# A gated mix of local attention and a GEGLU: attention's two layout changes, from DVE transposes to DMA transposes

## The chip, the core and the metric

The kernel runs on one core of one Trainium2 chip. The metric is the device time of one execution in microseconds (us), and the time of a version is the median over its runs. Engine names are those of the profile: PE does matmuls, DVE is the vector engine, ACT the scalar engine, POOL the general one, and SP issues DMAs. In profile rows, L844 is line 844 of the kernel.

## The reference

The input x has 2048 rows of 1024 numbers in bf16. Two branches are computed from it and mixed by a gate for each row:

```
g = sigmoid(sum(x * gate_w))                                  # one number a row
qkv = x @ wqkv; 32 heads of 32 numbers
for each row s, head h: keys and values of rows s, s-2, ..., s-14 (8 places, dilation 2)
    attn = softmax(q . k * 32**-0.5), places before row 0 masked
    o = sum(attn * v)
a = o @ wo
b = (gelu(x @ w_gate) * (x @ w_up)) @ w_down                  # 3584 wide
out = g * a + (1 - g) * b
```

## The kernel before, in words

**Tiling.** The 2048 rows go in four chunks of 512, two chunks to a superblock. All large products are made by a seven-product scheme for 2x2 blocks, so weights are needed raw and as sums (forms). PE works in this order: transposes of chunk 0's x, q, k and v of chunks 0 and 1 (L473), the FFN of superblock 0 (L970: 28 columns f, 28 matmuls each), down projection 0 (L1117, 252 matmuls; w_down and wo in one accumulation), q, k and v of chunks 2 and 3 (L609), down projection 1, the FFN of superblock 1, down projections 2 and 3.

**Evacuation in the FFN.** Each f leaves its banks by copies and gelus on ACT (L999, L1024, L1042, L1050, L1058, L1011) and by three DVE operations: L1054 adds two products of the gate path, L1033 two of the up path, L1014 multiplies them into hT. A late L1054 holds the gelu L1058 behind it, and with it all that follows on ACT.

**Attention** is done on DVE, between all this, in eight halves of 256 rows (h = 0 to 7, two to a chunk). Features lie so that each head has four of the 128 partitions, with eight features on each (the eight tiles t). For a half:

- `scores`: for each t, L781 multiplies q by the eight shifted k (128x2048), and L787 sums over t: 8 products and 7 sums. The last sum has the key ("qk", h).
- L844 transposes the 128x2048 sum in blocks of 32x32 (key ("acct", h)). L851 and L854 add the head's four partitions, which now lie side by side, L867 and L874 take the maximum, ACT does the exponential (L880), L867 the sum, L887 the reciprocal, L898 the probabilities in two pieces, and ACT spreads each over its features (L904).
- L913 transposes each piece back (2 x 128x1024). Then, for each t, L922 multiplies by the shifted v, and L930, L935 and L939 sum over the eight places into `qo`, which the down projection reads.

Since the blocks are 32x32, the scores lie as 4 groups of 32 partitions; the gate is kept in that layout too, and L756 copies it into columns of 128 rows (16 small copies in all). For h = 0, 28 memsets (L861) mask the places before row 0.

Five buffers (`xbuf`, 128x2048 each) serve all of this; a product is taken up only while a second buffer is free.

**Order.** One planner (`Weave`) writes the order of every engine at build time. It holds several streams of operations (the main one, loads, forms, `attention`, `scores`), each with a bias, keeps a clock for each engine from the cost written beside each operation, and always emits the head of the stream that could start first by that clock. Each engine then runs its list strictly in order. For a DMA the planner counts the issue on SP or POOL, the bytes over one common pipe, and 2.2 us until the data are there. In `scores`, the products of half h wait for ("acct", h - 1).

**Loads.** All loads are issued by SP in one list. Weights go into a ring of 20 buffers of 128x1024 (L342 for the FFN, L362 for the down projections, L307 for q, k, v): a load waits until PE has read what lay in its buffer. x of chunks 1 to 3 comes by DMA transposes (L313, eight a chunk, 128x512 each); those of chunks 2 and 3 stand in the list of loads behind weight blocks 9 to 12 of the first FFN (L384 to L386).

Of the kernel before, what the change touches and what calls it, by code (L numbers as in the profile page):

```python
# [40 lines left out]
class Weave:  # L41
# [42 lines left out]
    def _emit(self, op, t):  # L84
        cost = op.cost
        if op.eng == "ACT" and op.table is not None and op.table != self.table:
            self.table = op.table
            cost += 1.29
        if op.eng in ("SP", "POOL"):
            nbytes, issue = op.cost  # L90
            self.clk[op.eng] = t + issue
            self.pipe = max(self.pipe, t) + nbytes / self.RATE
            op.end = self.pipe + 2.2
        else:
            self.clk[op.eng] = t + cost
# [41 lines left out]
def kernel(  # L137
# [28 lines left out]
    assert H * DL == P and DL == 4 and KT == 8 and NCH % 2 == 0  # L166
    CW = NWIN * AC // DL
    CB = CW // NWIN
    SB = AC // 32
    HQ = 32 // DL  # L170
    FB = 2
    NBLK = FT // FB
    NW = D // 2
# [136 lines left out]
    def load_x(c, deps):  # L310
        deps = deps + ([[("acct", 1)], [("att", 0)]][c - 2] if c > 1 else [])
        for kt in range(KT):
            yield Op("SP", (P * SC * 2, 1.6), lambda kt=kt: nc.sync.dma_start_transpose(  # L313
                out=xT(c, kt), in_=x[c * SC:(c + 1) * SC, kt * P:(kt + 1) * P]), deps, key=("x", c, kt))

    def load_prep(i0):
        n = min(2, NPREP - i0)
        kind, src, nr = ("d", B_w_down, FH) if i0 < FH else ("o", A_wo, NTH)
        r0 = i0 if kind == "d" else i0 - FH
        si = i0 % 5  # L320

        def fn():
            st = stage(si)
            for h, r in ((0, r0), (1, nr + r0)):
                if kind == "d":
                    v = src[r * P:(r + n) * P, :].rearrange("(k p) (h n) -> p k h n", p=P, h=2)
# [39 lines left out]
    def loads():  # L366
# [14 lines left out]
            yield load_prep(i0)  # L381
        for b in range(2, NBLK):
            yield from load_block(0, b)
            if b >= XB:  # L384
                for c, k0 in ((2, 0), (2, 4), (3, 0), (3, 4))[b - XB:b - XB + 1]:
                    yield from list(load_x(c, []))[k0:k0 + 4]  # L386
        for sup in range(NSUP):
            c0 = 2 * sup
            more = sup + 1 < NSUP
# [319 lines left out]
    def gate(c):  # L709
# [20 lines left out]
        ez = small.tile([P, SC // 32], F32, tag="ez", bufs=2, name="ez")  # L730
        omg = small.tile([P, NST], F32, tag="omg", bufs=3, name="omg")
        gates[c] = (ez, omg, zq)

    def gate_sum(c):
        i, free = bank_take()
        zq = gates[c][2]

        def go():
            for q in range(4):
                nc.tensor.matmul(banks[i][32 * q:32 * (q + 1), 0:SC // 32], lhsT=qsum[:], rhs=zq[:], start=True, stop=True,  # L740
                                 tile_position=(0, 32 * q), skip_group_check=True)
        o = pe(1, go, [("zq", c)] + ([free] if free else []))
        yield o
        e = dve(0.1, lambda: nc.vector.tensor_scalar(out=zq[:], in0=banks[i][:, 0:SC // 32], scalar1=ZMAX, scalar2=-ZMAX,
                                                     op0=ALU.min, op1=ALU.max), [o], key=("zc", c))
        yield e
        bank_give(i, e)

    def gate_tail(c):
        ez, omg, og = gates[c]  # L750

        def tail():
            nc.vector.tensor_scalar(out=og[:], in0=ez[:], scalar1=1.0, scalar2=1.0, op0=ALU.mult, op1=ALU.add)
            nc.vector.reciprocal(out=og[:], in_=og[:])
            for q in range(4):
                nc.vector.tensor_copy(out=omg[32 * q:32 * (q + 1), :],  # L756
                                      in_=og[32 * q:32 * (q + 1), :].rearrange("p (j q) -> p j q", q=4)[:, :, q])
        yield dve(1.2, tail, [("ez", c)], lag=0.6, key=("omg", c))

    accs = {}  # L760

# [3 lines left out]
    def scores():  # L765

        for c in range(NCH):
            q_, k_ = qo[c % 2], kT[c]
            for a in range(SC // AC):
                a0 = a * AC  # L770
                h = (SC // AC) * c + a
                gate_ = [("acct", h - 1)] if h else []
                box, last = {}, {}

                def mult(t):
# [42 lines left out]
    def att_half(c, a, h):  # L818
# [10 lines left out]
        def flat(name):  # L829
            return xbuf[:, box[name], :]  # L830

        def lsb():
            return flat("z").bitcast(F32)[:, 0:CW].rearrange("p (w c) -> p w c", w=NWIN)

# [6 lines left out]
        def attn():  # L841
            return flat("w")[:, 3 * CW:4 * CW].rearrange("p (w c) -> p w c", w=NWIN)

        o = dve(2.24, taking("z", lambda: nc.vector.transpose(out=flat("z"), in_=xbuf[:, accs[h], :])), [("qk", h)],  # L844
                pre=xb_pre(), key=("acct", h))
        yield o
        xb_give(accs[h], o)

# [27 lines left out]
        yield o  # L876
        def exps():
            if a == 0:
                nc.scalar.activation(out=gates[c][0][:], in_=gates[c][2][:], func=ACT.Exp)
# [4 lines left out]
        if a == 0:  # L884
# [4 lines left out]
        o = dve(0.15, lambda: V(out=m4()[:, 2, :].rearrange("p (s h) -> p s h", s=SB),  # L889
                                in0=m4()[:, 1, :].rearrange("p (s h) -> p s h", s=SB),  # L890
                                in1=gates[c][0][:, a * SB:(a + 1) * SB].rearrange("p (s o) -> p s o", o=1)
                                .to_broadcast([P, SB, HQ]), op=ALU.mult), [("ez", c), o])
        yield o
        half = NWIN // 2
        es = []
# [14 lines left out]
        xb_give(box["w"], e)  # L910
        for i in range(2):
            def back(i=i):
                nc.vector.transpose(out=flat("ab")[:, i * n // 2:(i + 1) * n // 2],  # L913
                                    in_=flat("e")[:, i * n // 2:(i + 1) * n // 2])
# [372 lines left out]
```

## Time and profile before

| | |
|---|---|
| median of 5 runs | 732.35 us (731.22 to 733.67) |
| the profiled execution | 731.22 us, of which the span of its instructions is 729.4 us |
| granted PE clock | 1.000 |
| DMA moved | 163.73 MB, mean 224 GB/s |
| L844, a transpose of 128x2048 on DVE | 8 times, 2306 ns |
| L913, a transpose of 128x1024 on DVE | 16 times, 1225 ns |
| L781, L922, products of 128x2048 | 64 times each, 1217 and 1218 ns |
| PE, L970 of the FFN | 1568 matmuls |

The page first gives the busy time of each engine and its share of the span. Then it cuts the span into 40 slices of 18.2 us, with a digit for the tenths in which an engine was busy (9 is 90% or more), and the same for the 16 DMA engines. A row of a group tells the line, the engine, the operation, its tiles and shapes, how often it ran, its busy time and mean duration, and then the idle time of the engine just before it with what ended that time. A row of the waits reads "who <- waited for whom: us in total, times, longest". A row of the timeline gives the start, the duration, the engine, line and operation, and in brackets the engine's idle time before it and what ended it. Durations of neighbours on DVE overlap by some 0.07 us, so 128x2048 operations in a row start 1.14 us apart.

### The profile page before, as it was taken

How to read it: one execution, taken by the hardware profiler on the slowest of the kernel's cores; microseconds unless marked ns; L12 is line 12 of the kernel's file. 1: busy time of each engine (PE TensorE's matmuls, PEld its weight loads, DVE VectorE, ACT ScalarE, POOL GpSimd, SP SyncE). 2: the span in 40 equal slices, each digit the busy share in tenths (PEclk: the TensorE clock that was granted, in tenths of full speed). 3: DMA queues.
4: the chain of work that ended last, by engine and by line, in shares of the span. 5: the costliest groups of instructions: out<-in, count | busy, mean ns of one | idle time of the engine just before them, and what ended most of it. 6: DMA issues, size and time to landing. Idle time of an engine off the chain costs nothing.

```text
span 729.4 us, 9971 instructions
## 1 busy us (share of the span) xinstructions
PE 721.7 (99%) x3397; PEld 355.7 (49%) x3397; DVE 631.2 (87%) x935; ACT 314.6 (43%) x532; POOL 72.2 (10%) x128
## 2 busy tenths in 40 slices
PE   8999999999999999999999998999999999999998
PEld 6666644444444444456665443444444444444443
DVE  2689999999999989999899999999999999969300
ACT  2333455558555561035652113576557654220110
POOL 2234422121210100000000001000000000001000
PEclk9999999999999999999999999999999999999999
DMA  9999965648892769943029999555555544899993
GB/s 304 325 326 352 383 214 163 198 139 214 208 226 77 277 202 321 323 151 115 30 89 305 354 300 340 162 151 155 148 157 146 158 150 146 302 302 335 327 303 102
DMA packets 151507, 163.73 MB, mean 224 GB/s; under 512 B 22944, under 2 KB 112032, under 8 KB 151456
## 3 DMA queue, kind: packets, MB, share of 16 engines
q1 hardware_dynamic: 142624, 135.30, 61.4%
q0 software_dynamic: 8544, 27.27, 10.2%
q8 instruction: 26, 0.43, 0.2%
q10 hardware_dynamic: 288, 0.52, 0.2%
q14 instruction: 25, 0.20, 0.1%
HBM read 129.50 MB, written 28.31 MB: 216 GB/s over the span
## 4 chain that ended last, share of the span: by engine, by line
PE 73%; issue 21%; DVE 2%; ACT 1%; DMA 1%; POOL 1%; POOLq 0%; ACTq 0%
PE ps L970 45%; PE ps L1117 17%; PE ps L473 11%; DVE xbuf L922 1%; POOL out_dram L1144 1%; DMA hT<-in_A_x_dram 0%; DVE xbuf L930 0%; PE ps L1212 0%; DMA out_dram<-ost 0%; DVE xbuf L935 0%; DVE ost L1191 0%; ACT ost L1152 0%; ACT L1058 0%; DVE xbuf L787 0%; PE ps L717 0%
## 5 line engine op out<-in xcount | busy, mean ns | idle before, releaser
L970 PEld LDWEIGHTS <-ring 128*128 128x128 bf16 x1568 | 153.3, 98 | 187.8 <-issue 3.7
L970 PE MATMUL ps<-lend,ring 128*128 128x512 bf16 x896 | 212.3, 379 | 2.2 <-ACT m L1024 2.1
L970 PE MATMUL ps<-tf,ring 128*128 128x512 bf16 x672 | 164.0, 379 | 0.0
L1117 PE MATMUL ps<-ring,hT 128*128 128x512 bf16 x708 | 160.7, 379 | 0.0
L1117 PEld LDWEIGHTS <-hT 128*128 128x128 bf16 x708 | 69.2, 98 | 83.3
L781 DVE TENSOR_TENSOR xbuf<-qo,lend 128x2048 bf16<-128x2048 bf16 x64 | 77.3, 1217 | 2.3 <-ACT lend L495 2.3
L922 DVE TENSOR_TENSOR xbuf<-xbuf,lend 128x2048 bf16<-128x2048 bf16 x64 | 77.4, 1218 | 0.1
L787 DVE TENSOR_TENSOR xbuf<-xbuf 128x2048 bf16<-128x2048 bf16 x56 | 68.2, 1217 | 0.2
L609 PEld LDWEIGHTS <-ring 128*128 128x128 bf16 x336 | 43.9, 131 | 28.9 <-DMA ring<-in_A_wqkv_dram 0.4
L473 PE MATMUL ps<-lend,ring 128*128 128x512 bf16 x256 | 56.0, 380 | 0.2 <-DVE lend L1219 0.2
L999 ACT COPY ps<-ps 128x512 f32<-128x512 f32 x56 | 32.0, 571 | 54.8 <-PE ps L970 54.7
L1152 ACT ACTIVATE ost<-ps,omg 128x512 bf16<-128x512 f32 x16 | 11.0, 688 | 102.5 <-PE ps L1117 99.3
L1042 ACT ACTIVATE gl<-ps 128x512 bf16<-128x512 f32 x56 | 33.5, 598 | 49.8 <-PE ps L970 49.7
L1144 POOL DMA_DIRECT2D out_dram<-ost x24 | 13.0, 542 | 413.4 <-ACT ost L1152 319.4
L1117 PE MATMUL ps<-ring,qo 128*128 128x512 bf16 x192 | 49.3, 379 | 0.0
L473 PEld LDWEIGHTS <-ring 128*128 128x128 bf16 x256 | 36.7, 144 | 18.9 <-DMA hT<-in_B_w_down_dram 0.4
L443 POOL DMA_DIRECT2D fforms<-ring x56 | 30.5, 545 | 131.5 <-DVE ring L435 125.0
L609 PE MATMUL ps<-lend,ring 128*128 128x512 bf16 x192 | 43.5, 379 | 0.0
L1014 DVE TENSOR_TENSOR hT<-hT,gl 128x1024 bf16<-128x1024 bf16 x56 | 38.4, 686 | 5.7 <-ACT hT L1011 4.5
L930 DVE TENSOR_TENSOR xbuf<-xbuf 128x1024 bf16<-128x1024 bf16 x64 | 41.9, 686 | 0.7
L1054 DVE TENSOR_TENSOR u<-ps,u 128x512 f32<-128x512 f32 x56 | 38.4, 685 | 4.2 <-PE ps L970 3.2
L1033 DVE TENSOR_TENSOR hT<-ps,m 128x512 bf16<-128x512 f32 x56 | 38.4, 686 | 4.0 <-PE ps L970 3.9
(106 smaller groups left out, 724.5 us busy)
## 6 DMA issues: line engine op xcount, KB each, us to landing
ring<-dforms SPq DMA_DIRECT2D x112, 256.0 KB, 4.9
ring<-in_B_w_down_dram SPq DMA_DIRECT2D x84, 256.0 KB, 4.3
ring<-in_B_w_gate_dram SPq DMA_DIRECT2D x56, 256.0 KB, 4.9
fforms<-ring POOLq DMA_DIRECT2D x56, 256.0 KB, 4.8
ring<-fforms SPq DMA_DIRECT2D x56, 256.0 KB, 3.9
ring<-in_B_w_up_dram SPq DMA_DIRECT2D x42, 256.0 KB, 3.5
ring<-in_A_wqkv_dram SPq DMA_DIRECT2D x40, 256.0 KB, 4.5
ring<-oforms SPq DMA_DIRECT2D x32, 256.0 KB, 5.6
```

The source lines that it names most:

```text
L473: nc.tensor.matmul(banks[bk][:], lhsT=lhsT, rhs=xT(c, kt), start=(kt == 0), stop=(kt == KT - 1))
L609: nc.tensor.matmul(banks[bk][:], lhsT=lhsT, rhs=rhs[:, kt, :], start=(start and kt == 0), stop=(kt == KH - 1), skip_group_check=True)
L781: V(out=w3(box[t]), in0=q_b, in1=k_w, op=ALU.mult)
L787: V(out=w3(box[0]), in0=w3(box[0]), in1=w3(box[t]), op=ALU.add)
L922: return dve(tt(n), taking(("p", t), lambda: V(out=w3(box["p", t]), in0=w3(box["ab"]), in1=v_w, op=ALU.mult)), [("qkv", c, 2, t), abo] + ( ...
L930: V(out=s4(t)[:, t % 2], in0=w3(box["p", t])[:, 0:4], in1=w3(box["p", t])[:, 4:8], op=ALU.add)
L970: nc.tensor.matmul(banks[bk][:], lhsT=wv[:, k, fl * P:(fl + 1) * P], rhs=rhs[:, k, :], start=(start and k == 0), stop=(k == KH - 1), skip_ ...
L1014: yield dve(tt(2 * SC), lambda f=f: nc.vector.tensor_tensor(out=hT[:, :, f, :], in0=hT[:, :, f, :], in1=gl[f][:].rearrange("p (j s) -> p j ...
L1033: ev[f, "up2"] = dve(tt(SC, True), lambda f=f: nc.vector.tensor_tensor(out=hs(f, 1), in0=v3(banks[Bk[f]][:]), in1=v3(m5[f][:]), op=ALU.add ...
L1042: nc.scalar.activation(out=gl[f][:, SC:2 * SC], in_=banks[A[f]][:], func=ACT.Gelu_apprx_tanh)
L1054: e = dve(tt(SC, True), lambda f=f: nc.vector.tensor_tensor(out=u2[f][:], in0=banks[Dk[f]][:], in1=u2[f][:], op=ALU.add), [o, ev[f, "u2"]])
L1117: nc.tensor.matmul(banks[bk][:], lhsT=l, rhs=wv[:, i, :], start=(start and k == 0), stop=(q == last and i == 1), skip_group_check=True)
```

## The change

- The two layout changes of attention are made by DMA transposes, issued by SP (`turn`): one of 128x2048 as 16 blocks of 128x128, and two of 128x1024 back. L844 and L913 leave DVE. The planner is given an issue of 1.3 to 2.05 us for them and a tail behind the 2.2 us, 8 us in half 0 and 1.1 us in the others.
- A block is now 128x128, so a row s of the half is a partition. The mask of half 0 is 7 memsets, the gate has 4 columns instead of 16 and is made in the layout of the output (`gate_sum` gives each group of 32 partitions its own columns), and L756 is gone.
- The products of half h wait for ("qk", h - 1), the last sum of the half before, and not for its transpose.
- The x loads of chunks 2 and 3 leave the list of loads and form a stream of their own (`late_x`), four at a time behind the same blocks 9 to 12, still on SP.

Lines after the first edit shift by some: the fold is L856, L851 before; the FFN's L1054, L1033 and L1014 are L1058, L1037 and L1018; L922 is L926, L898 is L902; the transposes are L849 and L917; weight loads are L345 and L365.

```
-            op.end = self.pipe + 2.2
+            op.end = self.pipe + 2.2 + (op.tail if op.tail > 1.0 else 0.0)
...
-    SB = AC // 32
-    HQ = 32 // DL
+    SB = AC // P
...
+    def late_x():
+        for i in range(4):
+            yield from list(load_x(2 + i // 2, [("w", 0, XB + i, 3)]))[4 * (i % 2):4 * (i % 2) + 4]
...
             yield from load_block(0, b)
-            if b >= XB:
-                for c, k0 in ((2, 0), (2, 4), (3, 0), (3, 4))[b - XB:b - XB + 1]:
-                    yield from list(load_x(c, []))[k0:k0 + 4]
...
             for q in range(4):
-                nc.tensor.matmul(banks[i][32 * q:32 * (q + 1), 0:SC // 32], lhsT=qsum[:], rhs=zq[:], start=True, stop=True,
+                nc.tensor.matmul(banks[i][32 * q:32 * (q + 1), 0:NST], lhsT=qsum[:],
+                                 rhs=zq[:].rearrange("p (j q) -> p j q", q=4)[:, :, q], start=True, stop=True,
                                  tile_position=(0, 32 * q), skip_group_check=True)
...
-            nc.vector.tensor_scalar(out=og[:], in0=ez[:], scalar1=1.0, scalar2=1.0, op0=ALU.mult, op1=ALU.add)
-            nc.vector.reciprocal(out=og[:], in_=og[:])
-            for q in range(4):
-                nc.vector.tensor_copy(out=omg[32 * q:32 * (q + 1), :],
-                                      in_=og[32 * q:32 * (q + 1), :].rearrange("p (j q) -> p j q", q=4)[:, :, q])
-        yield dve(1.2, tail, [("ez", c)], lag=0.6, key=("omg", c))
+            nc.vector.tensor_scalar(out=omg[:], in0=ez[:], scalar1=1.0, scalar2=1.0, op0=ALU.mult, op1=ALU.add)
+            nc.vector.reciprocal(out=omg[:], in_=omg[:])
+        yield dve(0.3, tail, [("ez", c)], lag=0.6, key=("omg", c))
...
-                gate_ = [("acct", h - 1)] if h else []
+                gate_ = [("qk", h - 1)] if h else []
...
+        def rows(name):
+            return flat(name).rearrange("p (b s) -> p b s", s=P)
+
+        def turn(cols, fn, deps, **kw):
+            return Op("SP", (P * cols * 2, max(1.3, cols / 1000.0)), fn, deps, tail=8.0 if h == 0 else 1.1, lag=1.0, **kw)
...
-        o = dve(2.24, taking("z", lambda: nc.vector.transpose(out=flat("z"), in_=xbuf[:, accs[h], :])), [("qk", h)],
-                pre=xb_pre(), key=("acct", h))
+        o = turn(n, taking("z", lambda: nc.sync.dma_start_transpose(out=rows("z"), in_=xbuf[:, accs[h], :])), [("qk", h)],
+                 pre=xb_pre(), key=("acct", h))
...
-                for q in range(4):
-                    for wi in range(1, NWIN):
-                        nc.vector.memset(lsb()[32 * q:32 * q + DIL * wi, wi, 0:HQ], NEG)
-            o = dve(2.0, mask, [o])
+                for wi in range(1, NWIN):
+                    nc.vector.memset(lsb()[0:DIL * wi, wi, 0:H], NEG)
+            o = dve(0.5, mask, [o])
...
             def back(i=i):
-                nc.vector.transpose(out=flat("ab")[:, i * n // 2:(i + 1) * n // 2],
-                                    in_=flat("e")[:, i * n // 2:(i + 1) * n // 2])
-            o = dve(1.16, taking("ab", back) if i == 0 else back, [es[i]], lag=0.6, pre=xb_pre() if i == 0 else None)
+                nc.sync.dma_start_transpose(out=rows("ab")[:, i * NWIN:(i + 1) * NWIN],
+                                            in_=flat("e")[:, i * n // 2:(i + 1) * n // 2])
+            o = turn(n // 2, taking("ab", back) if i == 0 else back, [es[i]], pre=xb_pre() if i == 0 else None)
...
-    w.run([(0.0, main()), (0.0, loads()), (0.1, wforms()), (0.1, x_forms()), (0.1, qkv_forms()), (0.15, preps()), (0.3, attention()), (0.5, scores())])
+    w.run([(0.0, main()), (0.0, loads()), (0.0, late_x()), (0.1, wforms()), (0.1, x_forms()), (0.1, qkv_forms()), (0.15, preps()), (0.3, attention()), (0.5, scores())])
```

More of the change, by code (lines that the diff above doesn't have):

```diff
@@ L729, in gate @@
         yield e
-        ez = small.tile([P, SC // 32], F32, tag="ez", bufs=2, name="ez")
+        zc = small.tile([P, NST], F32, tag="zc", bufs=2, name="zc")
+        ez = small.tile([P, NST], F32, tag="ez", bufs=2, name="ez")
         omg = small.tile([P, NST], F32, tag="omg", bufs=3, name="omg")
-        gates[c] = (ez, omg, zq)
+        gates[c] = (ez, omg, zq, zc)
     def gate_sum(c):
         i, free = bank_take()
-        zq = gates[c][2]
+        zq, zc = gates[c][2:4]
         def go():
             for q in range(4):
-                nc.tensor.matmul(banks[i][32 * q:32 * (q + 1), 0:SC // 32], lhsT=qsum[:], rhs=zq[:], start=True, stop=True,
+                nc.tensor.matmul(banks[i][32 * q:32 * (q + 1), 0:NST], lhsT=qsum[:],
+                                 rhs=zq[:].rearrange("p (j q) -> p j q", q=4)[:, :, q], start=True, stop=True,
                                  tile_position=(0, 32 * q), skip_group_check=True)
@@ L743, in gate_sum @@
         yield o
-        e = dve(0.1, lambda: nc.vector.tensor_scalar(out=zq[:], in0=banks[i][:, 0:SC // 32], scalar1=ZMAX, scalar2=-ZMAX,
+        e = dve(0.1, lambda: nc.vector.tensor_scalar(out=zc[:], in0=banks[i][:, 0:NST], scalar1=ZMAX, scalar2=-ZMAX,
                                                      op0=ALU.min, op1=ALU.max), [o], key=("zc", c))
@@ L749, in gate_tail @@
     def gate_tail(c):
-        ez, omg, og = gates[c]
+        ez, omg = gates[c][0:2]
         def tail():
-            nc.vector.tensor_scalar(out=og[:], in0=ez[:], scalar1=1.0, scalar2=1.0, op0=ALU.mult, op1=ALU.add)
-            nc.vector.reciprocal(out=og[:], in_=og[:])
-            for q in range(4):
-                nc.vector.tensor_copy(out=omg[32 * q:32 * (q + 1), :],
-                                      in_=og[32 * q:32 * (q + 1), :].rearrange("p (j q) -> p j q", q=4)[:, :, q])
-        yield dve(1.2, tail, [("ez", c)], lag=0.6, key=("omg", c))
+            nc.vector.tensor_scalar(out=omg[:], in0=ez[:], scalar1=1.0, scalar2=1.0, op0=ALU.mult, op1=ALU.add)
+            nc.vector.reciprocal(out=omg[:], in_=omg[:])
+        yield dve(0.3, tail, [("ez", c)], lag=0.6, key=("omg", c))
     accs = {}
@@ L878, in exps @@
             if a == 0:
-                nc.scalar.activation(out=gates[c][0][:], in_=gates[c][2][:], func=ACT.Exp)
+                nc.scalar.activation(out=gates[c][0][:], in_=gates[c][3][:], func=ACT.Exp)
             nc.scalar.activation(out=lsb(), in_=lsb(), func=ACT.Exp, scale=scale)
@@ L891, in att_half @@
                                 in1=gates[c][0][:, a * SB:(a + 1) * SB].rearrange("p (s o) -> p s o", o=1)
-                                .to_broadcast([P, SB, HQ]), op=ALU.mult), [("ez", c), o])
+                                .to_broadcast([P, SB, H]), op=ALU.mult), [("ez", c), o])
         yield o
```

## The prediction

> **What bounds the kernel.** I read the page first, then who made PE wait, then the timeline around the one long wait, then the rows of the transposes that are there already. PE is the bound:
>
> ```profile
> span 729.4 us, 9971 instructions
> ...
> PE 721.7 (99%) x3397; PEld 355.7 (49%) x3397; DVE 631.2 (87%) x935; ACT 314.6 (43%) x532; POOL 72.2 (10%) x128
> ...
> DVE  2689999999999989999899999999999999969300
> ...
> DMA  9999965648892769943029999555555544899993
> ```
>
> PE is busy for 99% of the span, and DVE, at 87%, has no slack in most slices between the second and the 36th. DMA is full in the first 90 us and from slice 21 to 24 and 35 to 38. All of PE's waits:
>
> ```profile
> PE ps L970 <- ACT m L1024: 2.1, 1, 2.1
> PE ps L279 <- DVE hT L277: 1.2, 1, 1.2
> PE ps L1212 <- DMA hT<-in_A_x_dram: 0.6, 1, 0.6
> PE ps L473 <- DVE lend L1219: 0.2, 1, 0.2
> ```
>
> The last three lie in the start, which the change leaves alone. So one wait of 2.1 us is all that faster attention can give back. Its place, in order of time:
>
> ```profile
> 454.14 0.68 DVE L1054 TENSOR_TENSOR u<-ps,u 128x512 f32<-128x512 f32 x1
> ...
> 454.86 0.63 ACT L1058 ACTIVATE gl<-u 128x512 bf16<-128x512 f32 x1 [3.76 <-DVE u L1054]
> ...
> 455.40 0.57 ACT L1024 COPY m<-ps 128x512 f32<-128x512 f32 x1
> ...
> 456.01 0.38 PE L970 MATMUL ps<-lend,ring 128*128 128x512 bf16 x1 [2.06 <-ACT m L1024]
> ```
>
> At the start of the second FFN DVE is still multiplying values (L922 to L939 of half 4), so FFN's own L1054 comes late, ACT is held 3.76 us behind it, and PE stands 2.06 us. This also gives a tolerance: 3.76 - 2.06 = **1.7 us** of lateness on DVE in the FFN cost PE nothing.
>
> **What goes.** The transposes on DVE:
>
> ```profile
> L913 DVE STREAM_TRANSPOSE xbuf<-xbuf 128x1024 bf16<-128x1024 bf16 x16 | 19.2, 1225 | 4.0 <-ACT xbuf L904 4.0
> ...
> L844 DVE STREAM_TRANSPOSE xbuf<-xbuf 128x2048 bf16<-128x2048 bf16 x8 | 18.4, 2306 | 0.1
> ```
>
> That is 37.6 us. The 16 copies of L756 (160 ns) are 2.6 us; 28 memsets of L861, 0.75 us together, become 7, about 0.6 us. DVE loses 40.8 us of 631.2, some 4.7 us a half. None of it is on PE's path, except through the wait at 454 us: by then four and a half halves are done, so some 20 us of DVE work are gone ahead of it. The gate's narrower operations (16 to 4 columns) are too few to count; PE has as many instructions as before, in the same order.
>
> **What comes: 24 DMA transposes on SP.** Each has two parts, an issue on SP and a landing. The trace has no transpose from SBUF, and none this large. The nearest rows are the loads of x, 128x512 from HBM, a quarter of a turn of 2048 columns:
>
> ```profile
> 187.87 6.38 SPq L313 DMA_TRANSPOSE lend<-in_A_x_dram  x4
> ...
> L313 SPq DMA_TRANSPOSE lend<-in_A_x_dram x24: 1124/1282/2587, 25.9 to 217.7; - x24
> ...
> DMA to landing us min/median/max: 2.5/5.1/8.0
> ```
>
> Bounds for a turn of 2048 columns, issue to landing: at least 2.5 us (the quickest of a quarter of its size); at most 6.38 - 1.28 + 5.1 = 10.2 us, as if it were four in a row. It is nearest in bytes to the four, but has one issue instead of four: I take 8 us. For the pair of 1024 (L917 in the new code): 2.5 to 1.28 + 8.0 = 9.3 us after the first's issue; I take 1.28 + 5.1 = 6.4.
>
> [...]
>
> **Does DVE wait for a landing?** DVE runs in order, so a fold (L856 new) or a value product (L926) that waits also holds FFN's evacuations behind it. From the order of the changed kernel I summed DVE's work between the last sum of products (L786) and the fold, with the present rows (1.14 us a 2048-wide operation, 0.6 a 1024-wide one). Halves 0 to 7: 11.9, 8.9, 14.6, 40, **4.6**, 30, **7.0**, **1.8** us. Against 8 us, halves 4, 6 and 7 are short. Half 4 stands in the down projection, with no FFN evacuation behind it: 3.4 us of DVE idling, paid from the 20 us freed. Half 6 is 1.0 short, under the tolerance. Half 7 is short on paper by 6.2, but PE paces what stands around it: the evacuation behind the fold is due 6.05 us after the one ahead of it (one f of the FFN, 28 matmuls of 0.216), so it is late by 8 + 0.6 - 6.05 = 2.5 us at most, 0.8 over the tolerance, and by less for every moment that the last sum ends ahead of that first evacuation. For the way back, from the second probability product (L902) to L926: 14.8, 9.4, 7.2, 10.2, 9.9, 8.1, 8.1, 0 us, against a spread on ACT (1.05) and 6.4: 7.5. Half 2 is 0.3 short, in a down projection. Half 7 idles for all of it, with nothing of FFN behind it; its results (L939, the last at 669.7 us now) are read by down projection 3, whose 252 matmuls of 0.216 end at 725.8 and so begin at 671. I cost all this at 0.
>
> **SP's queue.** Behind each waiting turn stand the weight loads. In a down projection a ring buffer is freed in the second half of a product (18 of 36 matmuls) and is needed again two products on, 72 x 0.216 - 3.9 = 11.7 us later; a load lands in 5.5 us at the median there (391 to 445 us). So SP may be held 6.2 us at no cost; in the FFN, where a product's weights serve two f, it is more. A turn or a pair keeps SP issuing for four quarters at most, 6.4 us: it fits, just. The x loads of chunk 3 (8 x 1.28 = 10.3 us) move from 200 to 218 us into the first down loads, among which SP now waits 24.2 us for PE (230 to 262 us): 0. If that cover were gone they would cost up to 10.3 - 6.2 = 4 us.
>
> **DMA.** What the turns take of the engines, from three stretches (the last columns are DMA share and GB/s):
>
> ```profile
> 145.00:163.00 18.00, 18.00 (x85) 8.22 (x84) 17.62 (x22) 10.08 (x18) 2.90 (x6) 1.00 0.44 135
> 176.00:194.00 18.00, 18.00 (x85) 8.18 (x84) 17.85 (x27) 11.87 (x20) 2.71 (x5) 1.00 1.03 212
> ...
> 391.00:445.00 54.00, 54.00 (x252) 24.50 (x251) 53.28 (x74) 9.24 (x16) 3.79 (x7) 1.00 0.99 329
> ```
>
> Eight x transposes raise the share from about 0.5 to 1.03 over 18 us, some 1.1 us each, so a turn of 2048 takes up to 4.5 us of all engines. In 391 to 445 us, already at 0.99, one full turn and one pair fall: loads land up to 4.5 us later, inside the 6.2 us. 0, but thin.
>
> **Waiting for products only.** The next half's products (L780) no longer wait for the turn; that wait cost nothing before, since the transpose followed the last sum on DVE (0.1 us idle). It fills the landing. Taking it as 0 to 1 us, I take 0.
>
> **Sum.** The profiled execution took 731.22 us, span 729.4, and was the fastest of five; median 732.35. Less 2.06 that is 729.16 on its own time; on the median 730.3. All the PE spacings above 0.22 us beyond that wait sum to under 0.4 us, so 731.22 - 2.4 = 728.8 is the floor.
>
> **Forecast, 0.36: the stall goes, no new one comes: 730.3.** Own range 728.8 to 730.9.
>
> **Rival 1, 0.24: it does not do what it is to do: the stall stays, 732.4.** In the new order half 4's first two L926 still stand right ahead of the second FFN's first L1058 (the old L1054), and now need a landing. The pair's place on SP is behind the tenth FFN load, about 438 us in the old trace, where plain loads land in 6 to 8 us; with 1.28 for the second issue that is 446 to 448, and 2.9 us of products follow, up to 451. Another 3 us, and L1058 is as late as now. For it: DMA is full there. Against: DVE has 20 us less to do.
>
> **Rival 2, 0.28: slower, DVE caught behind late landings, 737.** If a turn takes the 10.2 us and a pair 9.3 + 1.05, then in the second FFN half 6's fold is late by 3.2, half 7's by 10.2 + 0.6 - 6.05 = 4.8, the pairs of halves 5 and 6 by 2.3 each. Less 1.7 each: 1.5 + 3.1 + 0.6 + 0.6 = 5.8 us; 732.35 + 5.8 - 2.06 = 736.1, or 738.2 with the stall at half 4 kept; between them 737. It decides from a landing 1.7 us over the windows, about 8.7 us at half 6. For it: DVE at 9 in nearly every slice. Against: the windows are sums of work alone; DVE's own waits lengthen them.
>
> **Rival 3, 0.12: weight loads late, about 754.** A turn waits on SP for DVE or ACT longer than 6.2 us with loads behind it. Six turns or pairs lie among down loads (halves 2, 3, 4, 7); at 4 us of PE idle each, 732.35 + 24 - 2 = 754. Against: SP stands for ring buffers most of that time anyway.
>
> **The numbers.** A measurement of this kernel can tell about 0.2%, 1.5 us, from no change. Faster by more: the forecast and a sliver of rival 1, 0.37. Within: rival 1 and the mildest of rival 2, 0.24. Slower: 0.39. The range leaves out rival 3 and reaches to rival 2 with its stall and the 4 us of the x loads: 728.8 to 742.
>
> **What would show it.** Right: DVE busy near 590 us, no PE wait over 1 us after 100 us, DVE waits "<-DMA xbuf<-xbuf" only outside the FFN. The turns' landing row tells 8 from 10 us. Wrong: PE L970 waiting for ACT L1028 or L1062 behind a DVE that waits for DMA xbuf (rival 1 or 2, by place), or PEld L1121 waiting for DMA ring (rival 3). Landings of 5 us or less would make me too cautious, of over 10 wrong.

## The result and the profile after

The changed kernel takes 735.78 us (median of 28 runs, 731.91 to 740.3) against 732.16 (49 runs): a ratio of **1.0047, 95% interval 1.0036 to 1.0057**, slower by 0.5%, where 730.3, faster than before, was forecast. The profiled execution took 736.16, span 734.4. The page of the changed kernel, and what its PE waited for (us in total, times, longest):

```profile
span 734.4 us, 9974 instructions
...
PE 723.1 (98%) x3397; PEld 355.9 (48%) x3397; DVE 592.3 (81%) x874; ACT 312.6 (43%) x530; POOL 72.3 (10%) x128
```

```profile
PE ps L974 <- ACT ps L1003: 5.4, 2, 3.8
```

DVE lost 38.9 us of work, near the 40.8 priced, and the 2.06 us wait at 454 us is gone. In its place PE waits 3.83 and 1.60 us for the seed copies (L1003) of the first FFN. The span cut at the first and the last matmul of each FFN, in us, in the profiled execution of every kernel (the names are explained under The experiments):

| kernel | to FFN 1 | FFN 1 | to FFN 2 | FFN 2 | rest | span |
|---|---|---|---|---|---|---|
| before | 92.5 | 177.8 | 174.9 | 179.6 | 104.6 | 729.4 |
| after | 92.2 | **184.9** | 175.1 | 177.6 | 104.6 | 734.4 |
| h0_tail20 | 93.5 | 181.2 | 184.6 | 178.1 | 104.6 | 742.0 |
| h0_after_block1 | 93.1 | 178.3 | 185.9 | 178.7 | 104.6 | 740.6 |
| h0_turn_on_dve | 92.7 | 177.5 | 175.1 | 177.6 | 104.7 | 727.6 |
| x_in_list | 91.9 | 194.2 | 174.8 | 177.4 | 104.6 | 742.9 |
| sp_swap | 92.7 | 185.3 | 175.7 | 177.6 | 104.6 | 735.9 |
| dve_same_plan | 93.0 | 177.4 | 174.9 | 177.7 | 104.8 | 727.8 |
| h0_turn_on_pe | 94.0 | 177.5 | 175.3 | 177.6 | 104.7 | 729.1 |
| gate_acct | 92.4 | 187.4 | 189.3 | 177.4 | 104.6 | 751.1 |
| idle_turn | 93.1 | 183.8 | 174.9 | 177.6 | 104.6 | 734.0 |
| two_preps_less | 92.4 | 177.5 | 175.6 | 177.6 | 104.6 | 727.7 |
| before_late_x | 91.8 | 177.6 | 174.9 | 177.4 | 104.6 | 726.3 |
| turns_twice | 92.5 | 184.2 | 190.5 | 203.6 | 110.1 | 780.9 |
| idle_copy | 92.3 | 178.1 | 174.9 | 177.6 | 104.6 | 727.5 |
| idle_half | 92.9 | 182.4 | 175.3 | 177.5 | 104.7 | 732.8 |

So the whole loss is in the first FFN: +7.1 us, of which 5.4 are the two waits; the second FFN gives 2.0 back. What happens ahead of that FFN is read engine by engine. SP of the changed kernel (start, duration of the issues, line, transfer, count):

```profile
63.54 5.58 SPq L849 DMA_TRANSPOSE xbuf<-xbuf  x1
69.23 1.19 SPq L345 DMA_DIRECT2D ring<-in_B_w_up_dram  x2
70.51 10.99 SPq L345 DMA_DIRECT2D ring<-in_B_w_gate_dram  x2
81.59 7.56 SPq L333 DMA_DIRECT2D hT<-in_A_wo_dram  x8
```

Half 0's turn holds SP for 5.58 us and lands after 16.36, at 79.9. Block 1's four loads stand behind it and land at 84.5 to 88.7 (before the change 70.0 to 75.3). DVE, in order, waits first for the one and then for the others (in brackets the idle time and its releaser):

```profile
79.92 0.69 DVE L856 TENSOR_TENSOR xbuf<-xbuf 128x1024 bf16<-128x1024 bf16 x1 [5.45 <-DMA xbuf<-xbuf]
87.22 0.69 DVE L435 TENSOR_TENSOR ring<-ring 128x1024 bf16<-128x1024 bf16 x1 [6.61 <-DMA ring<-in_B_w_up_dram]
...
94.62 0.69 DVE L878 TENSOR_TENSOR xbuf<-xbuf 128x512 f32<-128x512 f32 x1
```

Twelve microseconds of DVE are gone, and half 0's softmax (L878) comes at 94.6, when the FFN has begun. On ACT its exp and its spread stand ahead of the seed copies:

```profile
95.35 0.63 ACT L884 ACTIVATE xbuf<-xbuf 128x512 f32<-128x512 f32 x1 [8.04 <-DVE xbuf L878]
...
97.31 0.61 ACT L1003 COPY ps<-ps 128x512 f32<-128x512 f32 x1
...
105.30 1.04 ACT L908 COPY xbuf<-xbuf 128x1024 bf16<-128x1024 bf16 x1 [4.22 <-DVE xbuf L902]
```

and PE waits behind them:

```profile
97.97 1.02 PE L974 MATMUL ps<-lend,ring 128*128 128x512 bf16 x4 [3.83 <-ACT ps L1003]
...
106.88 0.38 PE L974 MATMUL ps<-lend,ring 128*128 128x512 bf16 x1 [1.60 <-ACT ps L1003]
```

The missing 7.1 - 5.4 = 1.7 us are slower matmuls: after the first wait the granted clock (third column from the right) is halved, in the trace from 99.11 to 102.52 us, and half of these 3.41 us is 1.7. Two windows of the changed kernel, inside that stretch and behind it, then the window of the 2.06 us wait before the change:

```profile
99.20:102.40 3.20, 3.20 (x10) 1.05 (x8) 3.06 (x9) 1.71 (x3) 2.19 (x4) 0.50 1.06 404
102.60:105.00 2.40, 2.40 (x19) 1.05 (x18) 2.30 (x7) 0.00 (x0) 1.17 (x3) 1.00 0.88 333
```

```profile
453.00:458.00 5.00, 2.94 (x15) 1.24 (x14) 4.93 (x9) 2.09 (x5) 0.00 (x0) 1.00 1.04 348
```

### The profile page after: what moved, and what is told of

Its sections match the earlier page's. It is cut to its first block, busy times and chain, and to the rows that moved or that the text cites. A ratio compares the mean times of both kernels' runs of the same rounds, so it can differ in the third digit from the quotient of the medians.

```text
span 734.4 us, 9974 instructions
## 1 busy us (share of the span) xinstructions
PE 723.1 (98%) x3397; PEld 355.9 (48%) x3397; DVE 592.3 (81%) x874; ACT 312.6 (43%) x530; POOL 72.3 (10%) x128
## 4 chain that ended last, share of the span: by engine, by line
PE 93%; DMA 3%; DVE 2%; ACT 1%; issue 1%; DVEq 0%; ACTq 0%
PE ps L974 44%; PE ps L1121 30%; PE ps L609 10%; PE ps L473 8%; DMA ring<-in_B_w_gate_dram 2%; DVE ring L435 0%; DMA hT<-in_A_x_dram 0%; PE ps L1216 0%; PE ps L717 0%; DVE hT L414 0%; DVE xbuf L871 0%; DVE hT L409 0%; ACT L1062 0%; DVE hT L412 0%; DVE xbuf L786 0%
## 5 line engine op out<-in xcount | busy, mean ns | idle before, releaser
L926 DVE TENSOR_TENSOR xbuf<-xbuf,lend 128x2048 bf16<-128x2048 bf16 x64 | 77.4, 1218 | 17.1 <-DMA xbuf<-xbuf 17.1
L780 DVE TENSOR_TENSOR xbuf<-qo,lend 128x2048 bf16<-128x2048 bf16 x64 | 77.3, 1218 | 2.2 <-ACT lend L495 2.1
L786 DVE TENSOR_TENSOR xbuf<-xbuf 128x2048 bf16<-128x2048 bf16 x56 | 68.2, 1217 | 0.3
L1003 ACT COPY ps<-ps 128x512 f32<-128x512 f32 x56 | 32.0, 572 | 52.9 <-PE ps L974 52.7
L1018 DVE TENSOR_TENSOR hT<-hT,gl 128x1024 bf16<-128x1024 bf16 x56 | 38.5, 687 | 12.5 <-ACT hT L1015 11.9
L1058 DVE TENSOR_TENSOR u<-ps,u 128x512 f32<-128x512 f32 x56 | 38.5, 688 | 9.1 <-PE ps L974 8.8
L473 PEld LDWEIGHTS <-ring 128*128 128x128 bf16 x256 | 36.6, 144 | 18.8 <-DMA hT<-in_B_w_down_dram 0.4
L435 DVE TENSOR_TENSOR ring<-ring 128x1024 bf16<-128x1024 bf16 x56 | 37.8, 683 | 8.3 <-DMA ring<-in_B_w_up_dram 8.0
```

Source lines behind the costliest of these rows:

```text
L435: nc.vector.tensor_tensor(out=g, in0=ring[:, held[("w", 0, b, x_)], :], in1=ring[:, held[("w", 0, b, y_)], :], op=op)
L473: nc.tensor.matmul(banks[bk][:], lhsT=lhsT, rhs=xT(c, kt), start=(kt == 0), stop=(kt == KT - 1))
L780: V(out=w3(box[t]), in0=q_b, in1=k_w, op=ALU.mult)
L786: V(out=w3(box[0]), in0=w3(box[0]), in1=w3(box[t]), op=ALU.add)
L926: return dve(tt(n), taking(("p", t), lambda: V(out=w3(box["p", t]), in0=w3(box["ab"]), in1=v_w, op=ALU.mult)), [("qkv", c, 2, t), abo] + ( ...
L1018: yield dve(tt(2 * SC), lambda f=f: nc.vector.tensor_tensor(out=hT[:, :, f, :], in0=hT[:, :, f, :], in1=gl[f][:].rearrange("p (j s) -> p j ...
```

## The experiments

The theories. **1**: half 0's steps wait for the late landing of its first turn, and on ACT they stand ahead of the seed copies. **2**: what the turn does to others, SP's hold and the crowded DMA engines, makes block 1's loads late; later split into 2a (the transposing form takes the engines' time) and 2b (any transfer there, or SP's wait). **3**: the 24 turns cost a little everywhere.

Each run's ratio is to the kernel before as measured beside it on the same chip. The runs come from four chips, on which the kernel before had medians of 731.7 to 732.2 us, so times of two runs may differ by 0.5 us for that alone.

| run | us, median (runs) | ratio to before, 95% interval |
|---|---|---|
| h0_tail20 | 745.62 (5) | 1.0194 (1.0171 to 1.0217) |
| h0_after_block1 | 742.39 (4) | 1.0140 (1.0121 to 1.0159) |
| h0_turn_on_dve | 729.38 (9) | 0.9966 (0.9954 to 0.9978) |
| x_in_list | 746.83 (6) | 1.0198 (1.0169 to 1.0226) |
| sp_swap | 738.57 (6) | 1.0087 (1.0072 to 1.0103) |
| dve_same_plan | 730.23 (9) | 0.9972 (0.9960 to 0.9983) |
| h0_turn_on_pe | 730.62 (12) | 0.9977 (0.9966 to 0.9988) |
| gate_acct | 754.62 (4) | 1.0303 (1.0283 to 1.0322) |
| idle_turn | 735.42 (6) | 1.0052 (1.0038 to 1.0066) |
| two_preps_less | 729.64 (10) | 0.9969 (0.9959 to 0.9980) |
| before_late_x | **728.53** (6) | 0.9961 (0.9948 to 0.9974) |
| turns_twice | 782.75 (4) | 1.0695 (1.0677 to 1.0714) |
| idle_copy | 731.45 (12) | 0.9996 (0.9979 to 1.0012) |
| idle_half | 734.47 (12) | 1.0032 (1.0016 to 1.0048) |

**Where is the loss?** First half 0's turn on another engine, then the planner told of a late landing, then the turn moved.

```diff
-        o = turn(n, ... nc.sync.dma_start_transpose(out=rows("z"), in_=xbuf[:, accs[h], :]) ...
+        if h == 0:
+            o = dve(2.24, ... nc.vector.transpose(out=flat("z"), in_=xbuf[:, accs[h], :]) ...
```

> Changed kernel with half 0's first turn made by DVE's 32x32 transposes (2.24 us planned) in place of the DMA, all other turns by DMA. The layout that follows is then not the one half 0's later steps assume, so half 0's attention is another computation of the same size. Theory 1 and theory 2: no wait for seed copies, 730; what is left of a difference to 729 would be the back turns of half 0. Theory 3 (23 of 24 turns are still there): 735.

729.38 (h0_turn_on_dve), and FFN 1 is back at 177.5. **Theory 3 falls as the cause**: with 23 of 24 turns in place the kernel isn't slower than before.

```diff
-  tail=8.0 if h == 0 else 1.1
+  tail=20.0 if h == 0 else 1.1
```

> Changed kernel with one number of the planner altered: the landing it reckons for half 0's three turns (8.0 to 20.0 us over the normal transfer). The DMAs are the same and SP still holds block 1's weight loads behind the first turn; but the planner now puts half 0's exps behind two of the seed copies on ACT instead of ahead of them. Theory 1 (the loss is half 0's late softmax standing ahead of seed copies in ACT's order): the PE waits of 3.83 and 1.60 us at 94 and 105 us go, and with them the dip of the granted clock; 736.2 less 5.4 less 1 gives about 730. Theory 2 (the loss is the weight loads of block 1, held on SP behind the turn, which leave DVE idle): the idle of DVE stays and the time stays near 735 to 736. Theory 3 (the turns' small packets cost something all along the kernel): at most 1 us is won.

745.62 (h0_tail20): no theory had that. By stages it still says something. With the exps behind two seed copies FFN 1 takes 181.2, half of the excess less: PE now waits 0.82, 1.75 and 0.81 us for other steps behind the same late DVE. The new order then loses 9.5 us elsewhere: at 413 us PE waits 4.93 us for DVE's L1089, which stands behind score products and sums (L780, L786). A hand-set delay reshuffles everything that follows, so such a run is read by stage only.

```diff
-  [("qk", h)], pre=xb_pre(), key=("acct", h))
+  [("qk", h)] + ([("w", 0, 1, 3)] if h == 0 else []), pre=xb_pre(), key=("acct", h))
-  gate_ = [("qk", h - 1)] if h else []
+  gate_ = [("acct" if h == 1 else "qk", h - 1)] if h else []
```

> Changed kernel with half 0's first turn planned only behind the forming of block 1's last weight form, so that SP issues block 1's loads first; the scores of half 1 wait for that turn as they did before the change (the five buffers would be full otherwise). Theory 1 (ACT's order): 730, as half 0's exps move behind four seed copies. Theory 2 (SP's hold): also 730, and DVE's idle of 6.6 us for w_up goes. Theory 3 (cost all along): 735 or more. Beside the run with the planner's number alone this tells theory 1 from theory 2: if both are near 730, the order is enough.

742.39 (h0_after_block1), again with a wait of 4.93 us at 412 us. FFN 1 is whole, 178.3. It does not tell 1 from 2, and as a time it settles nothing.

**The same with the order held.** The next six kernels keep the changed kernel's order on PE, ACT and POOL instruction for instruction, so a difference comes from what the edit itself moves.

```diff
   Op of the turn planned as before; what it emits:
+  if h == 0: nc.vector.transpose(out=flat("z"), in_=xbuf[:, accs[h], :])
+  else:      nc.sync.dma_start_transpose(out=rows("z"), in_=xbuf[:, accs[h], :])
```

> Changed kernel, planned with half 0's first turn as a DMA, so that the order on PE, ACT and POOL is that of the changed kernel, instruction for instruction; but the turn itself is made by one DVE transpose at its place, and SP issues nothing for it. Half 0's attention is then another computation of the same size, as the 32x32 layout is not the one its later steps assume. Theories 1 and 2: the data come in time, the same order on ACT does no harm: 729 to 731. Rival (the order the planner now makes for the start is bad by itself): 733 or more.

730.23 (dve_same_plan), FFN 1 177.4. The order on ACT, exps ahead of seeds, harms nothing when the data are in time.

```diff
   half 0's turn is emitted in the fn of the load ("w", 0, 1, "A12"), behind block 1's four loads
```

> Changed kernel with one thing exchanged: on SP, half 0's first turn is issued behind block 1's four weight loads instead of ahead of them. The order on PE, DVE, ACT and POOL is that of the changed kernel, instruction for instruction. Theory 1 (the turn's own late landing puts half 0's exps late, and they stand ahead of the seed copies on ACT): the turn lands later still, by 3 to 6 us, the waits of PE grow from 5.4 to 8 or more, 738 to 742. Theory 2 (block 1's loads, held behind the turn on SP, are what DVE waits for at 87 us): they land 5 us earlier, DVE's idle of 6.6 us goes and with it most of PE's 5.4 us: 730 to 732. If both the turn and the loads are late because the DMA engines are full, the exchange only swaps which one is waited for: 734 to 737.

738.57 (sp_swap), as theory 1 has it; the waits are 4.17 and 1.61 us. The turn, issued at 67.5, now holds SP for 11.82 us and lands after 20.2. One row of DVE (line numbers are 7 higher):

```profile
87.72 0.69 DVE L863 TENSOR_TENSOR xbuf<-xbuf 128x1024 bf16<-128x1024 bf16 x1 [14.03 <-DMA xbuf<-xbuf]
```

The loads came ahead of the turn, at 63.7 as in dve_same_plan, yet landed up to 81.1 instead of 73.3. So their lateness is not SP's hold alone.

```diff
+  if h == 0: DVE transposes into z, as in dve_same_plan; and
+      nc.sync.dma_start_transpose(out=<part of chunk 1's values, written later>, in_=xbuf[:, accs[h], :])
```

> The run with half 0's first turn on DVE in the changed kernel's own order (730.2 us), and in addition SP issues the same turn at the same place, into a part of the buffer of chunk 1's values that is written much later: the DMA and SP's hold are those of the changed kernel, but no step of half 0 waits for the landing. Half 0's attention and some of chunk 1's values are then another computation of the same size. Theory 1 (half 0's steps wait for the landing): 730 to 731. Theory 2 (the hold of SP and the crowding make other loads late): DVE still stands idle for block 1's w_up at 87 us, and 734 to 736 stays. In between, 732 to 733, both count.

**735.42 (idle_turn): nearly the whole loss, though no step reads what the turn brings. Theory 1 falls as the cause.** One step still waits for the turn, the fold, which writes over the buffer that the turn reads: 0.25 us. The late landing of the turn only decides which of two late things DVE meets first. Here it is the loads:

```profile
83.61 0.69 DVE L435 TENSOR_TENSOR ring<-ring 128x1024 bf16<-128x1024 bf16 x1 [6.20 <-DMA ring<-in_B_w_up_dram]
```

The last two columns of the windows 66 to 77 and 77 to 90 us, DMA share and GB/s, show why. dve_same_plan, then idle_turn, the changed kernel and sp_swap:

```profile
66.00:77.00 11.00, 11.00 (x52) 7.33 (x51) 10.93 (x15) 3.52 (x7) 5.38 (x9) 1.00 1.09 372
77.00:90.00 13.00, 13.00 (x62) 8.69 (x61) 10.51 (x24) 5.30 (x10) 6.57 (x11) 1.00 1.05 394
```

```profile
66.00:77.00 11.00, 11.00 (x53) 7.32 (x52) 10.68 (x14) 3.51 (x6) 4.41 (x8) 1.00 1.20 217
77.00:90.00 13.00, 13.00 (x62) 8.69 (x61) 5.36 (x17) 4.20 (x8) 4.85 (x9) 1.00 1.04 352
```

```profile
66.00:77.00 11.00, 11.00 (x53) 7.32 (x52) 8.40 (x12) 4.00 (x7) 3.90 (x7) 1.00 1.17 207
```

```profile
66.00:77.00 11.00, 11.00 (x53) 7.32 (x52) 7.62 (x12) 3.75 (x7) 6.01 (x10) 1.00 1.26 356
77.00:90.00 13.00, 13.00 (x62) 8.69 (x61) 2.28 (x4) 3.97 (x8) 0.66 (x2) 1.00 1.01 188
```

The engines are full in every row shown, but each run with the turn has a window in which they move 188 to 217 GB/s instead of 370 to 390. In the changed kernel (372 - 207) x 11 us = 1.8 MB fall out, 4.9 us of the full rate, for a turn of 0.5 MB. In sp_swap the gap moves with the turn.

```diff
-  for k in range(n):
+  for k in range(n if i0 not in (10, 12) else 0):
```

> Changed kernel, in which two of the nine loads of weights to be prepared (the ones issued before half 0's first turn, 8 DMAs of 256 KB, 2 MB) are left out; DVE prepares old data in their place, so two slices of the down projection's prepared weights are others. The order of all else is kept. Theory: the turn lands after 16 us because the DMA engines are full; at about 310 GB/s 2 MB are 6.5 us, so the turn lands after some 10 us, PE's waits shrink from 5.4 to under 2 us and the time to 729 to 732. Rival (this one turn is slow by itself, whatever lies before it): lands after 16 us still, 735 to 736.

729.64 (two_preps_less), as expected: with 2 MB less ahead of it the turn issues in 1.89 us and lands after 4.35, and PE has no wait in FFN 1. The turn is not slow by itself; it is slow where the engines are full. The time alone doesn't show that, since 2 MB less also lets block 1's loads land early (69.3 to 74.5 us); the landing of the turn does.

**Which part of the turn?** From idle_turn, the idle transfer alone is changed.

```diff
-  nc.sync.dma_start_transpose(out=idle..., in_=xbuf[:, accs[h], :])
+  nc.sync.dma_start(out=idle, in_=xbuf[:, accs[h], :])                          # idle_copy
+  nc.sync.dma_start_transpose(out=idle[:, 0:n // 2]..., in_=xbuf[:, accs[h], 0:n // 2])   # idle_half
```

> The run with the idle turn, in which a plain copy of the same 512 KB to the same place takes the turn's place on SP. The same steps of half 0 and values of chunk 1 are another computation. Theory 2a (the transposing form, whose stretch moved 217 GB/s where 372 went before, takes the DMA engines' time): 512 KB at about 370 GB/s are 1.4 us, DVE's idle for w_up is gone or under 1.5 us, 730 to 731. Theory 2b (any transfer put into this full stretch does it, or any wait of SP for half 0's products): 734 to 736 stays.

> The run with the idle turn, in which the turn has half its columns (1024 of 2048, 256 KB); otherwise the same. Theory 2a: half of the 5 us of lost transfer time, so DVE's idle for w_up falls from 6.2 to about 3 us, and 731 to 733. Theory 2b, or a cost of the turn that does not go by its size: 734 to 736.

The copy of the same bytes: 731.45, a little above the 730 to 731 expected; the rate in 66 to 77 us is 366, it holds SP for 0.55 us, and in the profiled execution, the shortest of its twelve, PE waits 0.6 us. So the form costs about 735.42 - 731.45 = 4.0 us: **2a**. The bytes at the same place cost 731.45 - 730.23 = 1.2, which the noise doesn't let tell from nothing (the intervals of the two runs overlap). The packets in the traces show what differs: the turn is 2048 packets of 256 B, which in idle_turn hold the 16 engines for 7.0 us (in the changed kernel for 5.9) when their times are added up (some overlap), the copy 128 packets of 4 KB and 1.4 us. The same 2048 packets take 2.8 us in two_preps_less. The half turn:

```profile
66.00:77.00 11.00, 10.95 (x52) 7.33 (x52) 10.88 (x15) 3.60 (x7) 5.38 (x10) 1.00 1.14 307
```

It loses (372 - 307) x 11 = 0.7 MB, under half of idle_turn's 1.7, but 734.47 is above the 731 to 733 expected. One PE wait of 2.67 us remains, and behind it the clock is halved for some 3.4 us (0.66 in the mean of 103 to 108 us), so that FFN 1 still takes 5.0 us more. In three of the twelve executions the mean clock shows no such fall (0.999 or 1.000), and these take 731.3 to 731.8 us, as expected; the other nine take 733.7 to 737.1. So the loss by size is near what was expected, and the clock lies on top of it. Why a packet of a turn takes so much longer where the engines are full stays open. So does the share of SP's issue time in the cost of the form: 5.19 us in idle_turn against 0.55 for the copy, 1.89 in the thinned queue and 11.82 in the fullest; it goes with the crowding and was not varied by itself.

**The other two parts of the change.** The loads of x back in the list of loads:

```diff
+            if b >= XB:
+                for c, k0 in ((2, 0), (2, 4), (3, 0), (3, 4))[b - XB:b - XB + 1]:
+                    yield from list(load_x(c, []))[k0:k0 + 4]
-    w.run([... (0.0, late_x()), ...
```

> Changed kernel with the loads of chunks 2 and 3 back in the list of loads, behind the loads of blocks 9 to 12, as before the change; the turns and the gate stay. Theories 1 and 2: the start is the same, so the time stays at 735 to 736. Rival (the stream of its own is what costs): back towards 731.

746.83 (x_in_list), wrong for all theories. Standing in the list, the x loads wait on SP for DVE's steps of attention, 27.4 us in all between 203 and 235 us, with weight loads behind them; at 240 us the order has the sums that prepare weights (L435 of the changed kernel) behind ten microseconds of half 2's score products and sums, and PE waits (line numbers are 3 higher):

```profile
250.56 1.89 PE L977 MATMUL ps<-tf,ring 128*128 128x512 bf16 x4 [10.07 <-DVE ring L438]
```

The old gate in the changed kernel:

```diff
-  gate_ = [("qk", h - 1)] if h else []
+  gate_ = [("acct", h - 1)] if h else []
```

> Changed kernel with the scores of the next half waiting for the turn again, as before the change, instead of for the products only. Theories 1 and 2: the turn of half 0 is as late, so 735 to 736 stays, give or take the 2 us by which another order of the later stages may differ; in the later FFNs DVE should stand idle for some turns. Rival (the gate lets scores of half 1 crowd out half 0's steps on DVE, which makes its exps late): 731 to 732.

754.62 (gate_acct), also wrong: with the products of half 1 behind a landing, DVE stands idle for 15.8 us up to 88.8 us, until block 1's w_up is there, and the later stages get another order. Without either part the changed kernel loses more, but in orders that differ all along. In the kernel before, the gate alone gives the same program. The stream alone:

```diff
+  late_x() as in the change, and its stream in w.run; the x loads taken out of loads()
```

> The kernel before with one part of the change alone: the loads of chunks 2 and 3 as a stream of their own. The planner's order on ACT, DVE and SP differs from the middle of the first FFN on. (The gate alone gives the old kernel instruction for instruction the same program, so it needs no run.) DVE keeps its 631 us. If the stall of 2.06 us at 454 us goes because DVE is lighter, it stays here: 731 to 733. Rival (the new stream removes the stall): 729.5 to 730.5.

**728.53 (before_late_x), the fastest of all**, faster than both kernels and below even the rival's 729.5 to 730.5. PE's 2.06 us wait at 454 us is gone though DVE keeps its work, as a line of the page and two of DVE's timeline show:

```profile
PE 720.3 (99%) x3397; PEld 354.6 (49%) x3397; DVE 631.0 (87%) x935; ACT 315.2 (43%) x532; POOL 72.0 (10%) x128
```

```profile
449.71 0.68 DVE L1055 TENSOR_TENSOR u<-ps,u 128x512 f32<-128x512 f32 x1
450.31 1.22 DVE L923 TENSOR_TENSOR xbuf<-xbuf,lend 128x2048 bf16<-128x2048 bf16 x1
```

The planner, with the x loads out of the list, put the FFN's L1055 (454.14 before) ahead of the last of these value products instead of behind it. By the stages of the profiled executions 3.1 us are won, of which 2.2 in FFN 2; 0.7 lie in the start, whose order the stream leaves alone. The freed DVE time was not run without the other parts. But in x_in_list, where the turns are there and the stream is not, the wait is gone too (FFN 2 takes 177.4). So it ends with either part of the change, each in an order of its own.

**Half 0's first turn on PE** (an identity kept in chunk 1's value buffer, 16 transposes in the second product group of chunk 1, two evacuations):

```diff
+  for k in range(8):                       # twice, into two PSUM banks
+      nc.tensor.transpose(out=pt[:, k, :], in_=xbuf[:, accs[0], (8 * i + k) * P:(8 * i + k + 1) * P], identity=ident)
+  (nc.vector.tensor_copy if i else nc.scalar.copy)(out=z, in_=pt)
```

> A version meant to keep the result: half 0's first turn by 16 TensorE transposes of 128x128 into two PSUM banks, evacuated by ACT and DVE; the other 23 turns by DMA. Nothing is issued on SP for it, and the order from the second product group on is that of the run with half 0's turn on DVE (729.4 us). The transposes in the first stage took PE 0.1 us or less each, so PE does 1 to 1.6 us more: 730 to 731, faster than both kernels by 1 to 2 us over the kernel before. Rival (any early layout change stalls PE): 733 or more.

730.62 (h0_turn_on_pe), as expected: faster than before, not than the stream alone.

**How much cover have the other turns?**

```diff
+  for _ in range(2 if h else 1):      # around each dma_start_transpose of halves 1 to 7
```

> The run with half 0's first turn on DVE in the changed kernel's own order (730.2 us), with every turn of halves 1 to 7 issued twice in a row into the same place: 21 turns more, about 17 MB of small packets. Each step that waits for a turn waits for the second one, some 4 to 7 us later. Theories 1 and 2 (the turns of halves 1 to 7 have cover): DVE's waits grow by some 40 us in all, but PE sees little of them, 730 to 734. Rival (turns cost wherever they are, a few tenths each): 735 to 745, spread over all stages.

782.75 (turns_twice), wrong by 50 us. The 21 turns more moved 7.3 MB (178.94 against 171.60 in dve_same_plan), not the 17 expected. The second of a pair writes where the first does, so SP stands for the first's landing (issued at 167.24, landed at 171.92, the second issued at 171.94), and the price is not of transfers alone. PE's waits of the run:

```profile
PE ps L980 <- DVE hT L1043: 12.2, 4, 4.8
PE ps L980 <- ACT m L1034: 9.6, 2, 8.6
PE ps L1127 <- DMA ring<-in_B_w_down_dram: 3.7, 3, 2.4
```

Late value products hold the FFN (DVE, ACT), and weight loads come late: the prediction's rivals 2 and 3, both, at a dose of twice the turns and more. One turn each fits; how much room there is between that and this dose was not run.

## Why the prediction was wrong

- **The failed step** is "DMA", with "SP's queue" beside it. The turns' 4.5 us of DMA time were weighed only from 391 to 445 us and put at 0; what half 0's turn does to the loads behind it in the first 90 us was put at nothing without a reason, though the same text said that DMA is full there. In its place the runs showed: the turn's DMA time with SP's hold made block 1's loads land 13 to 16 us later, DVE stood idle, half 0's softmax came late, and PE lost 7.1 us in FFN 1. The 4.5 us were near the right size (4.9 by the fall of the rate from 66 to 77 us); the place had no cover.
- "SP's queue" weighed the hold against the down projections alone, where PE in the changed kernel had no wait for a weight load; the hold in the start (5.58 us, then 10.99 for two loads) was not looked at.
- "Does DVE wait for a landing?" took half 0's window of 11.9 us as safe against 8 us. The window was read rightly, but the turn landed after 16.36. By idle_turn this miss is not what cost the time: the loss comes without it.
- That 735.78 lies in the stated range, near rival 2's 737, is luck. Rival 2 has its loss in the second FFN, at halves 5 to 7; that FFN takes 177.6 us, 2.0 less than before. No rival named the first. Rival 3, weight loads late behind a turn, is nearest in kind, but has them in the down projections.
- The turn's size: for halves 1 to 7 landing took 4.2 to 7.2 us, under the 8 taken, so rival 2 did not come. The pairs back took 4.9 to 9.8 us from the first's issue against the 6.4 taken, and PE did not wait for them. The row for all eight of L849 in the changed kernel:

```profile
DMA to landing us min/median/max: 4.2/5.9/16.4
```

  In the full stretch from 66 to 77 us the plain copy of the same bytes left the rate at 366 GB/s (idle_copy) and the turn in its place at 217 (idle_turn).
- The wait at 454 us went, as forecast, but that the freed DVE time is the reason is not shown. With the stream alone it goes at DVE 631.0, so less work on DVE isn't needed for it. Beside the stream the freed 38.9 us of DVE are worth nothing that could be measured: the rest of the span behind the start of FFN 1 is 634.5 us in before_late_x and 634.8 in dve_same_plan.
- "Waiting for products only", cost 0: right for the old kernel, where it changes no instruction; with the turns the kernel without it takes 754.62 - 735.78 = 18.8 us more, in another order.
- The x loads, cost 0: they cost nothing, and their stream alone gains 3.6 us. The prediction looked for gain only in the transposes.

Taken in this order, the change is a stream that wins (732.2 to 728.5), 23 turns with the gate that win and lose about nothing (730.23 against 728.53, with intervals that overlap), and one turn that loses 5.5 us (730.23 to 735.78).

## What to carry to other kernels

Price a transfer where it is placed: read the DMA share and the GB/s of that stretch, and count what it displaces, not its bytes. Time freed on an engine is worth only what the bounding engine waits for through it. Of a change in several parts, run each alone: here the part that looked like plumbing gave, by itself, more than the whole change was to give.

## What the runs showed of the hardware

- Beside full plain loads a DMA transpose of 0.5 MB within SBUF lowered the rate of all 16 engines from 372 GB/s (dve_same_plan) to 207 (the changed kernel) in the mean of the 11 us from 66 to 77, at a full DMA share (1.09 and 1.17); with 2 MB less ahead of it the same transfer landed in 4.35 us (two_preps_less). A plain copy of the same bytes left the rate at 366 (idle_copy).
- The granted clock was halved behind some waits of PE and not behind others. In the changed kernel, behind the wait of 3.83 us, it was 0.50 from 99.11 to 102.52 us, and the matmuls wholly inside started 0.43 us apart, against 0.22 behind it; behind the wait of 1.60 us it stayed at 1.00 (105 to 115 us). Behind a wait of 2.67 us it fell in idle_half (0.66 in the mean of 103 to 108 us) and in idle_turn (0.69 in the mean of 103 to 108 us, 0.97 of 108 to 113), in each for some 3.4 us. Behind another of 2.67 us, in x_in_list, it stayed at 1.00 (100 to 110 us), and so it did behind the 2.06 us wait of the profiled execution before the change (453 to 458 us). So in these runs the length of a wait alone does not tell whether the clock falls; what else decides it is not shown.
- What such a fall costs beyond the wait is, as an estimate, half of its 3.41 us, 1.7 us. Of 73 executions of the kernel before that were timed beside the experiments, 46 have a mean clock of 0.999 or 1.000 and take 731.4 us in the median, 27 have 0.997 or 0.998 and take 733.0. That would fit a wait of 2.06 us behind which the clock falls in some executions and not in others; the profiled execution alone shows the wait and the clock together, so this is not shown.
